# Fifteen small loads of one to fifteen partitions behind the last weight load of a decode step

## The chip, the cores and the metric

The kernel runs on one core of a Trainium2 chip. The metric is the device time of one execution in microseconds (us); of several runs the median is taken. All work is queued on the core's engines: TensorE (PE, with its weight loads as PEld), VectorE (DVE), ScalarE (ACT), GpSimd (POOL), and SyncE (SP), which here does nothing but issue transfers and wait. Sixteen DMA engines move the data between HBM and the on-chip memory SBUF.

## The reference

One decode step for one token: a layer norm, then attention over the last 4096 positions of a cache and, beside it, a two-layer perceptron, both added to the input.

```python
xn = _layernorm(x)                                   # x: 1 x 1 x 1024
# A: q = xn @ wq (1024 x 4096), 32 heads on 4 cache heads of the last W = 4096 positions
scores = einsum("bhqd,bhkd->bhqk", q, k) * Dh ** -0.5
o = einsum("bhqk,bhkd->bhqd", softmax(scores), v)
A = o.reshape(1, 1, 4096) @ wo                       # wo: 4096 x 1024
# B: y = _layernorm(xn)
B = gelu(y @ w1 + b1) @ w2 + b2                      # w1: 1024 x 3584, w2: 3584 x 1024
out = x + A + B
```

Everything is read once: with bf16 values, some 40 MB of weights and cache for 1024 outputs.

## The kernel before

**Tiles.** Every large array lands in one of four ring buffers of 32 KB in each of the 128 partitions: the cached keys (four loads, one for each cache head), wq in two halves, a scratch buffer for the transposed keys, w1 in two halves, the cached values (three loads), w2 in two halves, wo in two halves. A later tile takes the buffer that comes free first, and its load waits until the earlier tile's readers are done. Small tiles, the constants and the intermediate results, come from a pool with a place of its own for each (`consts`).

**Order of the work.** The keys are transposed on DVE (L189) and copied into place by ACT and DVE (L203, L205). TensorE multiplies by wq (L241) and w1 (L261), forms the scores (L279), the exponentials follow on ACT (L301), the values are weighted (L323), and then both output products run together into one accumulator `accf` (L344): 28 row blocks of w2 and 32 of wo, each block being one 128 x 1024 slice. The last four blocks of wo are taken apart from the others (`TAIL = 4`, L340) and go into two accumulators `acct` (L360), so that what has been summed until then can be copied out meanwhile (L348, L349). DVE and ACT make the result `res` (L364, L365), and two stores of 1 KB each end the kernel: the first half of the output is issued by SP (L367), the second by ACT (L368).

**The last loads.** The second half of wo is cut into five loads so that the last blocks arrive singly: blocks 0 to 7 (2048 KB), 8 to 11 (1024 KB), 12 and 13 (512 KB), 14 (256 KB), 15 (256 KB). They are the last five loads in the program (L232). After them SP has only its store of the output (L367) and the closing waits (L394).

**What sets the order in SP's queue.** All large loads and one store are issued by SP, one after another; an instruction whose wait isn't over holds up all that stands behind it. Three small loads (x, b2, b1) and the other store are issued by ACT. Two things decide what the waits are:

- A scheduler orders the instructions by a plan in which each engine takes, whenever it is free, the earliest instruction of the program that is ready. In its plan SP is taken up by each load for the time of its transfer. There SP goes from load to load without a gap from the first load of the keys to the last block of wo; the closing stores come 2.5 us of the plan later. The plan charges 0.5 us for a store of 1 KB. (These are times of the plan, not of the chip.)
- Each transfer reports its landing on one of eight completion counters, handed out in turn in the order of the plan, those of SP and ACT together. An instruction that takes a counter again first waits until the counter's previous transfer has landed, unless its engine has already waited for that. The order of the kernel before is:

```
counter 0: k head 0   then wq half 2    then wo half 1
counter 1: x          then w1 half 1    then wo half 2, blocks 0-7
counter 2: b2         then w1 half 2    then blocks 8-11
counter 3: k head 1   then v, first     then blocks 12-13
counter 4: b1         then v, second    then block 14
counter 5: k head 2   then v, third     then block 15
counter 6: k head 3   then w2 half 1    then ACT's store of the output
counter 7: wq half 1  then w2 half 2    then SP's store of the output
```

Two directives at the head of the kernel (`nc.vector.addr_align`, `nc.tensor.addr_align`) place the instruction streams of VectorE and TensorE on a multiple of 128 and of 256 instructions; SP has none.

Of the kernel before, what the change touches and what calls it, by code (L numbers as in the profile page):

```python
# [9 lines left out]
BF16 = mybir.dt.bfloat16  # L10
# [6 lines left out]
def kernel(  # L17
# [14 lines left out]
    nc = tc.nc  # L32
# [21 lines left out]
    consts = ctx.enter_context(tc.tile_pool(name="consts", bufs=1))  # L54
# [138 lines left out]
    for g in range(Hkv):  # L193
        T4 = scr[:, g, :].rearrange("p (c a j) -> p c a j", a=4, j=32)
        k = 0
# [30 lines left out]
    wo_v = A_wo.rearrange("(p c) n -> p c n", p=P)  # L226
    for i, cuts in enumerate([[0, 16], [0, 8, 12, 14, 15, 16]]):
# [4 lines left out]
            nc.sync.dma_start(out=tv[:, a:b, :], in_=wo_v[:, nr * i + a:nr * i + b, :])  # L232
        chunk_src += [("o", nr * i + r, tv[:, r, :]) for r in range(nr)]


    for i, w3 in enumerate(wq_tiles):
        for r in range(4):
# [161 lines left out]
```

## Time and profile before

| | |
|---|---|
| median of 2 runs | 101.78 us (101.76 to 101.79) |
| profiled execution, its own time | 102.08 us |
| its span | 100.3 us |
| share of the span that the DMA engines of SP's loads are busy | 93.4% |
| moved | 39.92 MB in 2878 packets, mean 398 GB/s |
| busy: PE, DVE, ACT, POOL | 47.9, 49.7, 34.1, 3.8 us |

The span is the stretch from the first to the last recorded instruction; the time of the same execution is 1.8 us longer. In the views of the queues, "SPq" is SP's instruction stream: a row of DMA_DIRECT2D is the time that SP spends to issue a transfer, not the transfer; EVENT_SEMAPHORE is an instruction that only waits. "Us to landing" runs from the start of the issue to the completion being seen. Waits name who waited, at which line, for whom, how long in total, how often, and the longest.

### The profile page before, as it was taken

The numbers are of one execution on the slowest core, as the hardware profiler recorded it, in microseconds if no ns is written. First come the engines' busy times: TensorE is split into PE (matmuls) and PEld (weight loads), VectorE is DVE, ScalarE is ACT, GpSimd is POOL, SyncE is SP. The second block draws the span as 40 slices with busy tenths as digits, with TensorE's granted clock in tenths as the row PEclk, the third lists the DMA queues.
The fourth block names the chain that finished last, engine by engine and source line by source line (L and its number), as shares of the span: only waits on it lengthen the run. The fifth ranks groups of instructions, "written<-read, shape, count | busy, mean of one in ns | idle before, by whom it ended". The sixth has DMA issues, their size and how long they took to land.

```text
span 100.3 us, 972 instructions
## 1 busy us (share of the span) xinstructions
PE 47.9 (48%) x365; PEld 19.0 (19%) x365; DVE 49.7 (50%) x92; ACT 34.1 (34%) x37; POOL 3.8 (4%) x16
## 2 busy tenths in 40 slices
PE   0028400004900680290594763999293920099990
PEld 0024200001200220020360221344041400032430
DVE  3614579999999999999423406240720000000021
ACT  5000000799999999991202024700000000000011
POOL 6000520000000000000000000000000000000000
PEclk9999999999997555559655588599999999655998
DMA  2999999999999999999899999999999999999910
GB/s 42 379 416 425 493 467 444 418 457 418 418 431 416 434 446 389 446 434 423 376 428 412 428 505 412 446 434 423 469 400 420 431 444 405 438 412 397 385 55 1
DMA packets 2878, 39.92 MB, mean 398 GB/s; under 512 B 309, under 2 KB 311, under 8 KB 698
## 3 DMA queue, kind: packets, MB, share of 16 engines
q1 hardware_dynamic: 2866, 39.85, 93.4%
q8 instruction: 3, 0.05, 0.2%
q10 hardware_dynamic: 8, 0.01, 0.0%
q14 instruction: 1, 0.01, 0.0%
HBM read 39.86 MB, written 0.00 MB: 397 GB/s over the span
## 4 chain that ended last, share of the span: by engine, by line
DVE 36%; DMA 28%; PE 18%; issue 10%; POOL 3%; POOLq 1%; ACT 1%
DMA wo<-in_A_wo_dram 28%; DVE kt_scr L189 17%; DVE kT L205 16%; PE accf L344 9%; PE sp L279 4%; PE acch L261 3%; DVE m_loc L287 1%; PE qT_ps L265 1%; PE acct L360 1%; DVE q_sb L244 1%; POOLq L394 1%; POOL spread L113 1%; ACT sc L284 1%; POOL rstd L148 1%; DVE res L364 0%
## 5 line engine op out<-in xcount | busy, mean ns | idle before, releaser
L203 ACT COPY kT<-kt_scr 32x1024 bf16<-32x1024 bf16 x26 | 27.1, 1042 | 16.2 <-DVE kt_scr L189 15.9
L189 DVE STREAM_TRANSPOSE kt_scr<-k_sb 128x4096 bf16<-128x4096 bf16 x4 | 17.4, 4412 | 0.0
L205 DVE COPY kT<-kt_scr 32x1024 bf16<-32x1024 bf16 x38 | 15.9, 419 | 0.5
L241 PE MATMUL accq<-wq,xnT 128*1 128x512 bf16 x64 | 7.2, 626 | 17.7 <-DMA wq<-in_A_wq_dram 17.7
L349 DVE COPY bulk<-accf 33x320 f32<-33x320 f32 x1 | 0.5, 482 | 23.0 <-ACT bulk L348 23.0
L344 PE MATMUL accf<-wo,o 128*1 128x512 bf16 x56 | 8.7, 484 | 6.6 <-DMA wo<-in_A_wo_dram 6.6
L348 ACT COPY bulk<-accf 33x192 f32<-33x192 f32 x1 | 0.3, 313 | 31.6 <-PE accf L344 31.6
L323 PE MATMUL o_all<-v_sb,eTb 128*32 128x512 bf16 x32 | 8.6, 438 | 1.1 <-DVE zcol L314 1.1
L261 PE MATMUL acch<-w,yT 128*1 128x448 bf16 x64 | 5.9, 542 | 4.9 <-DMA w<-in_B_w_dram 4.9
L344 PE MATMUL accf<-w,hT 128*1 128x512 bf16 x56 | 6.4, 379 | 1.7 <-DMA w<-in_B_w_dram 1.7
L241 PEld LDWEIGHTS <-xnT 128*1 128x1 bf16 x64 | 2.1, 116 | 22.0 <-issue 22.0
L344 PEld LDWEIGHTS <-o 128*1 128x1 bf16 x56 | 2.9, 101 | 12.4 <-issue 10.4
L323 PEld LDWEIGHTS <-eTb 128*32 128x32 bf16 x32 | 3.4, 110 | 5.9 <-issue 2.1
L279 PE MATMUL sp<-kT,qm 128*32 128x512 bf16 x32 | 3.8, 628 | 0.3 <-DVE qm L270 0.3
L126 PE MATMUL x_ps<-ones_bf,xb 1*128 1x1 bf16 x8 | 0.6, 197 | 6.4 <-DMA xb<-in_A_x_dram 6.4
L261 PEld LDWEIGHTS <-yT 128*1 128x1 bf16 x64 | 2.0, 115 | 8.8 <-issue 8.8
L344 PEld LDWEIGHTS <-hT 128*1 128x1 bf16 x56 | 2.3, 83 | 5.2 <-issue 1.9
L301 ACT ACTIVATE e<-sc,nmx 128x1024 bf16<-128x1024 f32 x1 | 1.1, 1147 | 5.1 <-DVE nmx L298 5.1
L318 DVE STREAM_TRANSPOSE hT<-h_sb 128x896 bf16<-128x896 bf16 x1 | 1.7, 1707 | 2.4 <-ACT h_sb L316 2.4
L326 DVE TENSOR_TENSOR o_m<-o_all,grs 32x512 f32<-32x512 f32 x1 | 0.7, 680 | 4.4 <-PE o_all L323 4.4
L265 PE MATMUL qT_ps<-ident,q_sb 128*128 128x128 bf16 x8 | 1.2, 306 | 3.3 <-DVE q_sb L244 3.3
L279 PEld LDWEIGHTS <-qm 128*32 128x32 bf16 x32 | 2.1, 132 | 1.4 <-issue 0.9
(88 smaller groups left out, 34.7 us busy)
## 6 DMA issues: line engine op xcount, KB each, us to landing
w<-in_B_w_dram SPq DMA_DIRECT2D x4, 3584.0 KB
wq<-in_A_wq_dram SPq DMA_DIRECT2D x2, 4096.0 KB, 26.6
k_sb<-in_A_k_cache_dram SPq DMA_DIRECT2D x4, 1024.0 KB, 8.1
wo<-in_A_wo_dram SPq DMA_DIRECT2D x1, 4096.0 KB, 28.6
v_sb<-in_A_v_cache_dram SPq DMA_DIRECT2D x1, 2048.0 KB, 18.8
v_sb<-in_A_v_cache_dram SPq DMA_DIRECT2D x2, 1024.0 KB, 22.7
wo<-in_A_wo_dram SPq DMA_DIRECT2D x1, 2048.0 KB
wo<-in_A_wo_dram SPq DMA_DIRECT2D x1, 1024.0 KB
```

The costliest lines, as they stand in the source:

```text
L113: nc.gpsimd.affine_select(out=spread[:], in_=spread[:], compare_op=ALU.not_equal, fill=1.0, base=0, pattern=[[-1, 4], [1, P]], channel_mul ...
L189: nc.vector.transpose(out=scr[:, g, :], in_=k2[:, g, :])
L203: nc.scalar.copy(out=dst, in_=src)
L205: nc.vector.tensor_copy(out=dst, in_=src)
L241: nc.tensor.matmul(accq[32 * t:32 * t + 1, b, :], lhsT=xnT[:, c:c + 1], rhs=w3[:, r, j * 512:(j + 1) * 512], start=(c == 0), stop=(c == C ...
L261: nc.tensor.matmul(acch[32 * t:32 * t + 1, b, :NH], lhsT=yT[:, c:c + 1], rhs=w3[:, r, j * NH:(j + 1) * NH], start=False, stop=(c == C - 1) ...
L265: nc.tensor.transpose(qT_ps[:, b * 4 + hh, :], q_sb[:, b, hh * Dh:(hh + 1) * Dh], ident[:])
L279: nc.tensor.matmul(sp[32 * R:32 * R + 32, :], lhsT=qm[:, g, :], rhs=kT[:, g, c0:c0 + 512], start=(g == 0), stop=(g == Hkv - 1), tile_posit ...
L301: nc.scalar.activation(out=e128[:], in_=sc[:], func=ACT.Exp, bias=nmx[:], scale=scale, accum_out=l_loc[:])
L318: nc.vector.transpose(out=hT[:], in_=h_sb[:].rearrange("p (d c) -> p c d", c=CW2))
L323: nc.tensor.matmul(o_all[:].rearrange("h g d -> h (g d)"), lhsT=eTb[:, 32 * c:32 * c + 32], rhs=v4[:, :, c, :], start=(c == 0), stop=(c == ...
L344: nc.tensor.matmul(accf[32 * half:32 * half + 1, :], lhsT=vec[kind](c), rhs=wap[:, half * 512:(half + 1) * 512], start=False, stop=(idx == ...
```

## The change

Behind the loads of wo, a tile `marks` of 16 partitions by 1536 bf16 columns is made in `consts`, and fifteen loads are issued on SP's queue. Load number k (1 to 15) brings k rows of 64 + 2k elements (132 to 188 bytes each), taken from the heads of rows 0, 32, 64 and so on of wo, into the first k partitions, at columns of its own. Nothing reads the tile. The text of the program is otherwise the same.

```diff
         for a, b in zip(cuts[:-1], cuts[1:]):
             nc.sync.dma_start(out=tv[:, a:b, :], in_=wo_v[:, nr * i + a:nr * i + b, :])
         chunk_src += [("o", nr * i + r, tv[:, r, :]) for r in range(nr)]
 
+    marks = consts.tile([16, 1536], BF16)
+    for k in range(1, 16):
+        w = 64 + 2 * k
+        nc.sync.dma_start(out=marks[0:k, 96 * k:96 * k + w], in_=wo_v[0:k, 0, 0:w])
+
 
     for i, w3 in enumerate(wq_tiles):
```

## The prediction

> **What bounds the kernel now.** The page's slices come first, then its chain:
>
> ```profile
> DMA  2999999999999999999899999999999999999910
> q1 hardware_dynamic: 2866, 39.85, 93.4%
> DVE 36%; DMA 28%; PE 18%; issue 10%; POOL 3%; POOLq 1%; ACT 1%
> ```
>
> The DMA engines are nine tenths busy or more in nearly every slice from 2.5 us to 95.3 us. The kernel is a stream of loads with a short tail, and a change counts by what it does to the stream or to the tail. The 20 KB that are added (rows of 132 to 188 bytes, 120 of them) are nothing to the stream: at 398 GB/s they take 0.05 us. So the tail, and SP's queue:
>
> ```profile
> SPq L367 <- DVE res L364: 25.2, 1, 25.2
> SPq L84 <- DMA k_sb<-in_A_k_cache_dram: 3.0, 1, 3.0
> ```
>
> ```profile
> 72.09 0.91 SPq L232 DMA_DIRECT2D wo<-in_A_wo_dram  x2
> ```
>
> ```profile
> 98.22 0.31 SPq L367 DMA_DIRECT2D out_dram<-res  x1
> ```
>
> SP issues its last load at 72.57 (the second of the two issues that end at 73.00; it takes 0.43) and its store at 98.22, and waits 25.2 us between. By this row alone fifteen more issues would be free. The second wait row says otherwise: the load of the second half of wq needs nothing of the keys, yet it stands 3.0 us for a load of keys, because it takes that load's completion counter. The fifteen loads take counters too, and those belong to the loads of wo, which are still on their way. When these land:
>
> ```profile
> wo<-in_A_wo_dram SPq DMA_DIRECT2D x1, 4096.0 KB, 28.6
> wo<-in_A_wo_dram SPq DMA_DIRECT2D x1, 512.0 KB, 24.4
> wo<-in_A_wo_dram SPq DMA_DIRECT2D x2, 256.0 KB, 24.7
> ```
>
> The first half of wo was issued at 58.97 and lands at 87.53, blocks 12 and 13 at 71.62 + 24.4 = 96.0, block 15 at 72.57 + 24.7 = 97.27. For the two pieces without a landing I divide by the stream's rate: 2048 KB in 5.3 us lands about 92.8, 1024 KB in 2.6 us about 95.4.
>
> **Which load waits for what.** In the scheduler's plan SP has no gap before the last block of wo, so that nothing can be moved ahead of it: the loads stay behind block 15, at 0.5 us of the plan each. ACT's store comes in that plan 2.5 us after block 15, that is behind the sixth load. Counted on from counter 5 (block 15), loads 1 to 6 take counters 6, 7, 0, 1, 2, 3, ACT's store 4, loads 7 to 15 take 5, 6, 7, 0, 1, 2, 3, 4, 5, and SP's store takes 6. Each waits for the previous owner:
>
> - load 1: first half of w2, landed by 72.98, when TensorE starts on it without a wait. Issued at 73.0.
> - load 2: second half of w2. The row below has SP's next instruction begin at 77.8, when that half is in. Issued at 77.8.
> - loads 3 to 6: 87.5, about 92.8, about 95.4, 96.0.
> - load 7: block 15, 97.27.
> - loads 8 to 13: loads 1 to 6. These lie in the same queues behind wo, whose last packets pass by 97.0, and should have landed by the time SP comes to each.
> - load 14: ACT's store. It is issued at 98.24, and the closing wait for it is over at 99.3.
> - load 15: load 7. SP's store: load 8.
>
> ```profile
> L367 SPq EVENT_SEMAPHORE  x1: 20404/20404/20404, 77.8 to 77.8; - x1
> ```
>
> ```profile
> L394 SPq EVENT_SEMAPHORE  x1: 28/28/28, 99.3 to 99.3; - x1
> ```
>
> So the first six loads are hidden in the 25.2 us, and loads 7 to 15, nine of them, are issued from 97.3 on, ahead of the store that before went out at 98.22. Of the nine issues the first 0.95 us (97.27 to 98.22) is covered by the last matmuls and the two instructions that make `res`; the rest delays the store, and the store is the last thing in the kernel: from its issue to the end of the span are 2.08 us, before and after.
>
> **The price of one issue** is the term that the trace doesn't show for such a load. On SP back to back, with 128 partitions, starts lie 0.46 to 0.48 apart (the issues at L232: 0.425 to 0.433 each, with 0.04 between). On ACT, one partition, the second load in a row takes 0.22 and the third starts 0.25 after it:
>
> ```profile
> 1.67 0.50 ACTq L105 DMA_DIRECT2D xb<-in_A_x_dram  x1
> 2.21 0.22 ACTq L106 DMA_DIRECT2D xb<-in_B_b_dram  x1
> 2.46 0.34 ACTq L107 DMA_DIRECT2D b_row<-in_B_b_dram  x1
> ```
>
> SP's store, one partition after a pause, takes 0.31 where ACT's takes 0.22, so SP is rather the dearer of the two. Ends: 0.25 and 0.475. The nine loads have 7 to 15 rows, between the two rows in size, on SP and back to back as the upper one: I take 0.38, a little above the middle. 9 x 0.38 = 3.42, and 0.03 for a separate wait instruction ahead of the store, since that has three things to wait for. The store is issued at 97.27 + 3.45 = 100.72, which is 2.5 us late. Load 14 is reached at 97.27 + 7 x 0.38 = 99.93, after ACT's store has landed, so it waits for nothing. ACT's own store waits for block 14's counter and keeps its place.
>
> The sum is 102.08 + 2.5 = 104.58 for the profiled execution; that one lies 0.3 above the median of the runs, so for the median 101.78 + 2.5 = 104.3 us, 2.5% slower. Nothing is removed, so nothing is gained. TensorE and VectorE run the same instructions; the small tiles behind `marks` and the ring lie 3 KB further on in each partition, a price that no row shows, which I put at nothing, within 0.1 us either way.
>
> [...] The issue rows at L232 are 0.425 to 0.433 for 128 partitions, but 0.22 for one. [...]
>
> **The rivals.**
>
> *Cheap issues: 103.4 us.* If SP issues these loads at ACT's 0.25, load 14 is reached at 97.27 + 1.75 = 99.02 and waits until 99.3 for ACT's store; loads 14 and 15 take 0.5, the wait 0.03, and SP's store goes out at 99.85, 1.6 late. ACT's row speaks for it, SP's 0.31 for a store against. The verdict turns at 2.04 us, an issue of 0.33 (9 x 0.33 + 0.03 = 3.0; 97.27 + 3.0 = 100.27).
>
> *Issues at one price whatever the size: 105.0 us.* At 0.465 the nine take 4.19, the store goes out at 101.49, 3.3 late. The L232 and L75 rows on the same queue speak for it, the short one-row issues against. [...]
>
> *Not slower: 101.8 us.* The store isn't delayed, because the loads don't wait for counters of wo and all pass in the pause: fifteen issues of at most 0.475 are 7.1 us, from 73.0 to 80.1, far below 98.22. It decides as soon as load 7 can be issued 2.5 us or more before 97.27 (the 3.45 us of the sum then end by 98.22). For it: the 25.2 us pause. Against it: the 3.0 us that wq's load stands for the keys.
>
> *Slow landings: about 106 us.* Each of loads 8 to 15 and the store stands behind a transfer of the same tail. If a small load takes 2 us or more from issue to landing (the two stores take 1.1 and 1.3), or one of the DMA engines lags, waits add to issues: 1 to 2 us more. The first two landings of keys (6.1 us at best) are of a full stream and say little.
>
> **How the numbers follow.** Forecast 0.57, cheap issues 0.17, one price 0.13, not slower 0.07, slow landings 0.05, a gain from somewhere (the moved tiles) 0.01. The range goes from under the cheap case, 103.1, to over the one-price case, 105.5; it leaves out 0.07 + 0.05 + 0.01 and a little of the edges. About 2% (2.04 us) is what a measurement of this kernel can tell from no change. Slower by more: the forecast but for its low edge (0.53), one price and slow landings, 0.71. Within: cheap issues, not slower and that edge, 0.28. Faster: 0.01.
>
> **What will show it.** In the profile after: SP's issues of the new line, six of them spread from 73 to 96 and nine in a row from 97.3; SP's wait of 25.2 us at L367 gone, and in its place waits of the new line for loads of wo, some 9.4 us for the first half (78.1 to 87.5) among them; the store's issue near 100.7; ACT's store still at 98.2. TensorE, VectorE and the loads of wo should stand where they stood. If the store's issue is at 98.2, the counters were read wrongly; if the nine issues lie apart with waits of the new line for itself or for the output, the landings are slow.

## The result and the profile after

The changed kernel takes 104.40 us in the median of two runs (104.39 and 104.40) against 101.78 before: a ratio of 1.0258, 95% interval 1.0213 to 1.0302. That is 2.6 us more. The profiled execution has a span of 102.7 us, 2.4 more than before.

The page first: the DMA engines' slices, SP's queue, and the chain.

```profile
DMA  2999999999999899998999999999899998999200
q1 hardware_dynamic: 3106, 39.87, 91.5%
DVE 35%; DMA 28%; PE 17%; issue 10%; POOL 3%; POOLq 1%; ACT 1%
```

The stream of loads is as full as before (the slices are of 2.57 us now), and the chain has the same parts: it ends at the making of `res`, so the new loads aren't in it, and what they cost has to be read in SP's queue. The queue has 3106 packets instead of 2866: 240 more, which is one for each of the 120 rows and as many again. I read the second 120 as one for each DMA engine of each load; the runs with sixteen rows and seventeen take this up. The time lies behind the stream. Here are the waits of SP's queue (who, at which line, for whom: total, how often, longest); L238 is the line of the new loads, L399 that of the closing waits:

```profile
SPq L238 <- DMA wo<-in_A_wo_dram: 18.3, 5, 9.6
...
SPq L238 <- DMA w<-in_B_w_dram: 4.4, 1, 4.4
...
SPq L399 <- DMA marks<-in_A_wo_dram: 0.8, 2, 0.4
```

The one wait of 25.2 us for `res` is gone. In its place the new loads wait once for w2 and five times for wo, 22.7 us together, and no wait of a new load for another new load is in the view. The timeline of the same queue, cut into short windows (start, time, engine, line, and how many issues are merged):

```profile
72.78 0.33 SPq L238 DMA_DIRECT2D marks<-in_A_wo_dram  x1
77.53 0.25 SPq L238 DMA_DIRECT2D marks<-in_A_wo_dram  x1
87.43 0.24 SPq L238 DMA_DIRECT2D marks<-in_A_wo_dram  x1
92.28 0.25 SPq L238 DMA_DIRECT2D marks<-in_A_wo_dram  x1
94.72 1.49 SPq L238 DMA_DIRECT2D marks<-in_A_wo_dram  x2
...
98.27 0.23 ACTq L373 DMA_DIRECT2D out_dram<-res  x1
100.61 0.24 SPq L372 DMA_DIRECT2D out_dram<-res  x1
```

Loads 1 to 5 go out at 72.8, 77.5, 87.4, 92.3 and 94.7, the sixth at 95.94 (the second of the last row of loads: it ends at 96.21). ACT's store leaves at 98.27, as before; SP's store at 100.61 instead of 98.22. Between stand loads 7 to 15. The view of line 238 in windows gives the price of each (count, then shortest, median and longest in ns, then first and last start); the first of the nine and the last:

```profile
L238 SPq DMA_DIRECT2D marks<-in_A_wo_dram x1: 268/268/268, 97.2 to 97.2; - x1
...
L238 SPq DMA_DIRECT2D marks<-in_A_wo_dram x1: 382/382/382, 100.1 to 100.1; - x1
```

From 7 to 15 rows the issues take 268, 296, 291, 313, 328, 344, 362, 367 and 382 ns, 2.95 us together, with 0.04 between: SP is busy from 97.2 to 100.5 without a pause. The closing waits of SP (line 399), in two windows:

```profile
L399 SPq EVENT_SEMAPHORE  x1: 28/28/28, 101.4 to 101.4; - x1
L399 SPq EVENT_SEMAPHORE  x3: 28/28/28, 101.8 to 101.9; - x3
```

The counters that these waits name in the trace show which is which. The wait at 101.4 is over when load 14 has landed (issued at 99.7), the first of the three at 101.8 when load 15 has (issued at 100.1): both took about 1.7 us. The next, for SP's store, is over at once: the store needed at most 1.3. So the store had landed no later than load 15, or within 0.1 us of it; the run with both stores on ACT's queue takes this up.

### The profile page after: what moved, and what is told of

The parts are those of the page before. It is cut to its first block, busy times and chain, and to the rows that moved or that the text cites. A ratio compares the mean times of both kernels' runs of the same rounds, so it can differ in the third digit from the quotient of the medians.

```text
span 102.7 us, 987 instructions
## 1 busy us (share of the span) xinstructions
PE 47.8 (47%) x365; PEld 19.2 (19%) x365; DVE 49.7 (48%) x92; ACT 34.1 (33%) x37; POOL 3.8 (4%) x16
## 3 DMA queue, kind: packets, MB, share of 16 engines
q1 hardware_dynamic: 3106, 39.87, 91.5%
## 4 chain that ended last, share of the span: by engine, by line
DVE 35%; DMA 28%; PE 17%; issue 10%; POOL 3%; POOLq 1%; ACT 1%
DMA wo<-in_A_wo_dram 28%; DVE kt_scr L189 17%; DVE kT L205 16%; PE accf L349 9%; PE acch L266 3%; PE sp L284 3%; DVE m_loc L292 1%; PE qT_ps L270 1%; PE acct L365 1%; DVE q_sb L249 1%; POOLq L399 1%; POOL spread L113 1%; ACT sc L289 1%; POOL rstd L148 1%; DVE res L369 0%
## 5 line engine op out<-in xcount | busy, mean ns | idle before, releaser
L284 PE MATMUL sp<-kT,qm 128*32 128x512 bf16 x32 | 2.9, 502 | 0.4 <-DVE qm L275 0.4
```

Of the source, the lines that this page charges most:

```text
L284: nc.tensor.matmul(sp[32 * R:32 * R + 32, :], lhsT=qm[:, g, :], rhs=kT[:, g, c0:c0 + 512], start=(g == 0), stop=(g == Hkv - 1), tile_posit ...
```

## The experiments

Ratios are to the kernel before on the same chip in the same series, where its median was 102.03 us (102.05 for the runs with ten loads, the reverse order, sixteen rows and seventeen); "more" is the difference of those medians.

**Six loads.** Only the loads that lie in the pause, with the tile as large as in the change.

```diff
-    for k in range(1, 16):
+    for k in range(1, 7):
```

> The tile as before, but only loads 1 to 6; the other nine loads are left out. Theory (nine issues that stand behind the landing of block 15): all six issues lie in SP's pause, the store's counter is that of block 15, which has landed; nothing is late, 101.8 us, SP's store issued at 98.2 to 98.3. Rival (the moved tiles, or the mere presence of small transfers in the queues of wo): part of the 2.6 us stays, 102.3 us or more.

Measured: 102.18 us, ratio 1.0023 (0.9999 to 1.0046). The store is issued when `res` is there. The view of the store's line has the wait ahead of it, and the timeline the store:

```profile
L372 SPq EVENT_SEMAPHORE  x1: 885/885/885, 97.1 to 97.1; - x1
```

```profile
98.01 0.24 SPq L372 DMA_DIRECT2D out_dram<-res  x1
```

This wait begins when block 15 has landed, whose counter the store takes here, and lasts 0.89 us until `res` is there: it is the cover, measured, and nothing used it. Neither the tiles that moved by 3 KB nor small transfers in the queues of wo cost anything clear of the noise (0.15 us, and the interval reaches from nothing to 0.5).

**Ten loads.**

```diff
-    for k in range(1, 16):
+    for k in range(1, 11):
```

> Loads 1 to 10; the last five are left out. Theory (each issue behind block 15 costs its price once the cover is used up): four issues stand behind block 15, 0.27 + 0.30 + 0.29 + 0.31 and gaps of 0.04 make 1.33, less 0.95 of cover, so SP's store goes out 0.4 late; load 10 is issued about 98.3 and lands 1.7 later, about 100.0, where the store landed at 99.5 before. 0.4 to 0.5 us more than the kernel before. Rival (the cost goes with the number of loads, 10 of 15): 1.7 us more.

Measured: 102.57 us, ratio 1.0046 (1.0014 to 1.0079), 0.5 more. In the timeline the store goes out at 98.60:

```profile
98.60 0.24 SPq L372 DMA_DIRECT2D out_dram<-res  x1
```

So ten loads cost 0.5 us and fifteen 2.6: the first six are free, four more nearly so, and the last five cost 2.1. That is the shape of issues behind a cover of about 1 us, and not of a price for each load.

**All fifteen, six of them ahead of the second half of wo.**

```diff
+        if i == 1:
+            for k in range(10, 16):
+                w = 64 + 2 * k
+                nc.sync.dma_start(out=marks[0:k, 96 * k:96 * k + w], in_=wo_v[0:k, 0, 0:w])
         nr = CWO // 2
...
-    for k in range(1, 16):
+    for k in range(9, 0, -1):
```

> All fifteen loads, but loads 10 to 15 stand ahead of the second half of wo and loads 9 down to 1 behind block 15. By the order of the counters the early six wait for w1, v and w2; blocks 0 to 7 of wo are issued at 77.8 instead of 70.8 (the second half of w2) and the four other pieces from 87.5, which is before the queues have run through what stands ahead of them; of the late nine only the last three (3, 2 and 1 rows) wait for block 15. Theory: three issues of 0.24 and gaps of 0.04 from 97.3 end at 98.1, under the cover of the last matmuls: 101.8 us, at most 102.0. Rival (it is the traffic of the 120 rows, or the number of issues as such): 104.4 us. If the queues of wo run dry at 87.5, the loads of wo land later and it is slower than 102.0, with a gap in the DMA share about 88 to show it.

Measured: 102.30 us, ratio 1.0044 (1.0018 to 1.0071): 0.3 more than before, a little above what was expected, with the same 120 rows and, on SP's queue, the same 3106 packets as the change. The slices of the DMA engines, from the page, show no gap at 88 us (slice 35 of 40):

```profile
DMA  2999999999999999999899999999999999999910
```

although the timeline has the pieces of wo (line 237 here) issued late:

```profile
77.91 0.36 SPq L237 DMA_DIRECT2D wo<-in_A_wo_dram  x1
87.67 1.77 SPq L237 DMA_DIRECT2D wo<-in_A_wo_dram  x4
...
98.42 0.23 ACTq L377 DMA_DIRECT2D out_dram<-res  x1
98.43 0.24 SPq L376 DMA_DIRECT2D out_dram<-res  x1
```

Six early issues and the order of the rest take away 2.3 of the 2.6 us. The traffic is not the cause, and neither is the number of issues as such: what counts is how many stand behind the landing of block 15, three here and nine in the change. In this execution the three delay nothing: SP's store goes out together with ACT's, which stands behind no load. `res` itself is 0.2 later than before (stores at 98.42 and 98.43 against 98.22 and 98.24), since block 15 lands 0.2 later (97.5 against 97.3). Whether that comes from the later issues of wo stays open: in the other profiles, all with wo issued earlier, block 15 lands anywhere from 97.0 to 98.3.

**Both stores on ACT's queue.** The store passes the fifteen loads.

```diff
-    nc.sync.dma_start(out=out_v[0:1, :], in_=res[0:1, :])
+    nc.scalar.dma_start(out=out_v[0:1, :], in_=res[0:1, :])
```

> All fifteen loads as in the change; the first store of the output is issued by ACT instead of SP, so that it passes the loads. Theory A, as predicted (the store is late because it stands behind nine issues, and nothing else matters): the stores go out at 98.3 and 98.5, 102.1 us. Theory B, after the profile of the change (the last load is issued at 100.1 and lands at 101.8, as late as the store does, and the closing waits want both): 104.2 to 104.4 us, although both stores land near 99.7.

Measured: 104.28 us, ratio 1.0229 (1.0195 to 1.0263), 2.25 more. The timeline of ACT's queue has the two stores 0.3 apart, near the old place:

```profile
98.54 0.24 ACTq L372 DMA_DIRECT2D out_dram<-res  x1
98.81 0.26 ACTq L373 DMA_DIRECT2D out_dram<-res  x1
```

Line 238 has the issue of the last load,

```profile
L238 SPq DMA_DIRECT2D marks<-in_A_wo_dram x1: 382/382/382, 100.5 to 100.5; - x1
```

and the waits of SP's queue have the closing waits for the new loads:

```profile
SPq L399 <- DMA marks<-in_A_wo_dram: 0.8, 2, 0.5
```

Theory A of this run falls. The stores are out 1.8 us earlier than SP's in the change, and the kernel ends as late, because the closing waits want the landing of the last load, which nobody reads.

**One row in each load.**

```diff
-        nc.sync.dma_start(out=marks[0:k, 96 * k:96 * k + w], in_=wo_v[0:k, 0, 0:w])
+        nc.sync.dma_start(out=marks[0:1, 96 * k:96 * k + w], in_=wo_v[0:1, 0, 0:w])
```

> Fifteen loads of the same widths, each of one row only. The price of an issue in the profile of the change goes from 0.24 (2 to 4 rows) to 0.38 (15 rows). Theory (the end is nine issues, and the price of one goes with its rows): 0.24 and 0.04 for each, load 14 is reached at 99.2 and waits until 99.35 for ACT's store, load 15 is issued at 99.6 instead of 100.1, 103.9 us. Rival (one price, or the landings set the pace): 104.4 us.

Measured: 103.81 us, ratio 1.0177 (1.0144 to 1.0211), 1.8 more. The issues take 222 to 253 ns, but for the first. And the wait that the prediction put into its case of cheap issues is there, among the waits of SP's queue:

```profile
SPq L399 <- DMA marks<-in_A_wo_dram: 0.4, 2, 0.3
SPq L238 <- DMA out_dram<-res: 0.4, 1, 0.4
SPq L399 <- DMA out_dram<-res: 0.2, 1, 0.2
```

Load 14 waits 0.4 us for ACT's store, whose counter it takes. The last of the closing waits is for the store here: load 15, of one row, takes only 1.2 us to land (99.97 to 101.15) and is in before it. Without the wait of load 14 the store would go out earlier and the gain from cheaper issues be larger by as much; this is argued, no run shows it.

**The reverse order.** Fifteen rows first, one row last.

```diff
-    for k in range(1, 16):
+    for k in range(15, 0, -1):
```

> All fifteen loads in the reverse order, 15 rows first and 1 row last, so that the six dear ones are hidden in the pause and the nine behind block 15 have 9 to 1 rows. Theory: the nine take 2.36 of issues and 0.36 of gaps instead of 3.26; load 14 is reached about 99.4, when ACT's store is just about landed; the last load is issued near 99.7, 0.4 earlier than in the change, so 2.0 to 2.2 us more than the kernel before instead of 2.6. Rival (one price, or the traffic of the rows): as the change.

Measured: 103.94 us, ratio 1.0196 (1.0149 to 1.0243), 1.9 more, against 2.6 for the change in its own series. The profiled execution is the slowest of the six (105.02 us; its load 7 is issued at 98.3), so only distances inside it are used: from the issue of load 7 to that of the last load there are 2.6 us, against 2.9 in the change.

```profile
L238 SPq DMA_DIRECT2D marks<-in_A_wo_dram x1: 272/272/272, 98.3 to 98.3; - x1
L238 SPq DMA_DIRECT2D marks<-in_A_wo_dram x1: 250/250/250, 100.9 to 100.9; - x1
```

The direction is as expected, and the 0.3 is what the cheaper issues of the last nine save in that execution; the last load, of one row, also lands sooner, in 1.2 us. The interval is too wide for more. The issues in between don't fall evenly with the rows: 0.29 to 0.30 from eight rows down to four, then 0.27, 0.25 and 0.25.

**Sixteen rows and seventeen.** What makes an issue dear, the rows or the DMA engines?

```diff
-    marks = consts.tile([16, 1536], BF16)
+    marks = consts.tile([17, 1536], BF16)
...
-        nc.sync.dma_start(out=marks[0:k, 96 * k:96 * k + w], in_=wo_v[0:k, 0, 0:w])
+        nc.sync.dma_start(out=marks[0:17, 96 * k:96 * k + w], in_=wo_v[0:17, 0, 0:w])
```

(Shown for 17; with 16 the tile keeps its 16 partitions.)

> Fifteen loads of 16 rows each. Both theories of the price (it goes with the rows, or with the DMA engines that a load is spread over, as many as it has rows up to 16) give 0.24 + 12 x 0.0145, about 0.40, and 0.04: the last load is issued at 97.3 + 8 x 0.44 = 100.8, 0.7 later than in the change, 3.0 to 3.4 us more than the kernel before. It is the base for the next run.

> Fifteen loads of 17 rows each. [...] Theory R (the price goes with the rows): 0.42 an issue, as with 16 rows or a little more, 3.1 to 3.5 us more than the kernel before.

Measured: with 16 rows 104.98 us, ratio 1.0284 (1.0244 to 1.0323), 2.9 more; with 17 rows 104.21 us, ratio 1.0227 (1.0176 to 1.0278), 2.2 more. With 16 rows, the page's packets on SP's queue and, from the view of line 238, the last of the issues:

```profile
q1 hardware_dynamic: 3346, 39.89, 91.0%
```

```profile
L238 SPq DMA_DIRECT2D marks<-in_A_wo_dram x1: 417/417/417, 100.6 to 100.6; - x1
```

The same two with 17 rows:

```profile
q1 hardware_dynamic: 3136, 39.89, 91.9%
```

```profile
L238 SPq DMA_DIRECT2D marks<-in_A_wo_dram x1: 278/278/278, 99.6 to 99.6; - x1
```

Against the 2866 of before there are 480 packets more with 16 rows (15 x 32) and 270 with 17 (15 x 18), as there were 30 more with one row (15 x 2). So beside its rows a load has one small packet with one row, sixteen with sixteen and one with seventeen. In the kernel before, each of the 19 loads of 128 rows has sixteen: the page counts 309 packets under 512 bytes, all rows there are larger, and five of the 309 go with the three small loads and the two stores, one each as with one row, which leaves 304.

```profile
DMA packets 2878, 39.92 MB, mean 398 GB/s; under 512 B 309, under 2 KB 311, under 8 KB 698
```

The views count sixteen DMA engines, and I read one small packet as one engine; the trace doesn't name the engine of a packet. So read, seventeen rows went through one engine. One row more makes the issue a third cheaper (0.417 us and 0.278). The theory that the price goes with the engines holds, with one of them at seventeen rows, and theory R falls; the 16-row run came out just under its range. So the price, back to back, goes with the engines and hardly with the rows: 0.25 for one row on one engine, 0.28 (the median) for seventeen rows on one, 0.42 for sixteen on sixteen, 0.43 for 128 on sixteen (line 232 before).

The landing takes part of this back. With seventeen rows the store is issued 3.0 us after load 7 (97.0), and the last closing waits for the loads and the store are over 1.4 us after that:

```profile
99.97 0.24 SPq L372 DMA_DIRECT2D out_dram<-res  x1
```

```profile
L399 SPq EVENT_SEMAPHORE  x2: 28/28/28, 101.4 to 101.5; - x2
```

In the one-row run the store is issued 3.0 us after load 7 too, with the wait of load 14 among them, and yet the kernel with seventeen rows takes 0.4 us more: its last load lands after 1.6 us instead of 1.2, and its store after 1.4 instead of 1.1. That the rows queue on the one engine is a likely reason; no run shows it.

## Why the prediction was right

It gave 104.3 us, 103.1 to 105.5, and the median is 104.40. The mechanism was right up to the store's issue, and the end was right by luck. By its own steps:

- **The order of the counters** was right, load by load. Loads 1, 2, 3 and 6 were put at 73.0, 77.8, 87.5 and 96.0 and came at 72.8, 77.5, 87.4 and 95.9. The two that were worked out from the mean rate, 92.8 and 95.4, came at 92.3 and 94.7: the stream was faster there than its mean. Load 7, the one that matters, was put at 97.27 and came at 97.2.
- **Nine issues ahead of the store** was right. The price was taken as 0.38 with the pause between two of them; measured are 0.27 to 0.38, 0.33 in the mean, and 0.04 between, so 0.37. That the guess hit so well is partly luck: it was a value near the middle of two rows, and nothing in it said that the price goes with the DMA engines, of which these nine loads, as read from the packets, use eleven in the mean. The 0.31 of SP's store, which made SP look the dearer, is no rule either: the same store takes 0.24 in the profile after. The store's issue was put at 100.72 and came at 100.61.
- **The cover of 0.95 us** held: it measures 0.89 with six loads, and ten loads cost 0.5, where the sum of four issues less 0.95 gives 0.4.
- **"The store is the last thing in the kernel"** is the step that failed, and by luck without harm to the sum. Load 15 is issued 0.5 us before the store and takes about 1.7 us to land, the store at most 1.3, and so they land together; nothing in the prediction made that so, and with one row in each load the store lands last after all. With both stores out of the way the kernel still took 104.28. The price of the change has two carriers that end at one time, and the prediction named one.
- **The rivals.** *Cheap issues* was right on what it would be like (one row: 0.25 an issue, and the wait of load 14 for ACT's store), wrong for the loads of the change. *One price whatever the size* falls: the same queue issues at 0.25 and at 0.42. Its 0.465 is near what back-to-back issues on sixteen engines take with the pause between them (0.42 to 0.43, and 0.04). *Not slower* falls by the waits at line 238 for wo. *Slow landings* falls: the last loads take about 1.7 us to land, not 2, and no load waited for another, because between two of them on one counter lie 2.9 us and more (load 7 at 97.2, load 15 at 100.1). What it had in view, a small load that lands later than a store, is there, and it puts load 15 at the end.
- **Within 0.1 us for the moved tiles:** six loads with the whole tile, 1.0023 (0.9999 to 1.0046), don't contradict it; the interval is too wide to show it.

## What to carry to other kernels

In a program built like this one, a transfer that nobody reads still has to be issued in its queue (0.24 to 0.38 us for each load of the change), may have to wait for the counter that it takes (22.7 us in all for w2 and wo), and has to land before the kernel may end (104.28 us, though both stores were issued by 99.1); behind a long stream of loads the first transfers to take the counters of that stream are held until it lands (load 7 until 97.2), and all that follows in the queue with them. Before putting small transfers behind a stream, count the completion counters and see whose they are: here fifteen loads cost 2.6 us behind the last load, and 0.3 when six of them stand ahead of the second half of wo. For small transfers that must stand near the end, fewer engines, as read from the packets, made a cheaper issue (seventeen rows on one engine 0.28 us and 104.21 for the kernel, sixteen on sixteen 0.42 and 104.98), though seventeen rows on one engine landed later than one row (1.6 us against 1.2).

## What the runs showed of the hardware

The issue of a transfer on SP's queue, back to back, took 0.25 us on one DMA engine (engines as read from the small packets), 0.29 to 0.30 on four to nine, 0.38 on fifteen and 0.42 on sixteen, near enough whatever the rows (0.28 in the median for seventeen on one engine, 0.43 for 128 on sixteen). Right behind a wo load of 128 rows the first small load took longer than that, 0.33 with one row and 0.48 with fifteen, but with sixteen hardly so, 0.43. The first issue after a wait was cheaper in these cases: 0.31 to 0.32 instead of 0.42 with sixteen rows (loads 2, 3 and 7 of that run), 0.22 instead of 0.25 with one; one such issue, load 3 with seventeen rows, took 0.81 for a reason that was not found.

From the start of its issue until SP's closing wait for it was over, behind the stream's end, the last small load (rows under 200 bytes) took 1.2 us with one row and 1.5 to 1.7 with fifteen, sixteen or seventeen; the 1 KB stores took 1.1 to 1.4. A queue that was issued its next pieces about 5 us before it would run dry (an estimate: 2048 KB at the 398 GB/s of before; blocks 8 to 15 of wo from 87.67 on, while blocks 0 to 7 were passing) showed no gap.
